# A recurrence and two feed-forward layers on one core: weights joined in place, five buffers for unit inputs, and eight units' u term on the matrix engine

## The chip, the cores and the metric

One NeuronCore of one Trainium2 chip. The metric is device time in microseconds (us) of one launch. Engines are named TensorE (PE; PEld is its weight load), VectorE (DVE), ScalarE (ACT), GpSimd (POOL) and SyncE (SP), which issues most DMAs.

## What is computed

A recurrence over 768 steps for 4 batches and 8 heads of width 48, then two feed-forward layers over the 3072 tokens (384 to 2048 to 384), the first gated by a leaky ReLU with a slope per column, the second by h * relu6(h + 3) / 6.

```python
def _attn_ref(r, k, v, w, u):
    ...
    for t in range(S):
        cur = np.einsum('bhd,bhe->bhde', u[None] * kt, vt)
        y[:, :, t] = np.einsum('bhd,bhde->bhe', rt, state + cur)
        state = wt[:, :, :, None] * state + np.einsum('bhd,bhe->bhde', kt, vt)

def _moe_ref(x, w_in, w_out, alpha):
    h = x @ w_in
    g = np.maximum(h, 0.0) + alpha * np.minimum(h, 0.0)
    return g @ w_out
```

r, k, v, w and u are fp32. The four weight matrices arrive as 64-bit floats and are turned into 32-bit ones on the chip. The u term of a step is, per head, the number sum_d(r*u*k) times the vector v.

## The kernel before

The tokens are cut into 12 thirds of 256 (three to a batch), and each third into four units, one for each pair of heads: 48 units. A unit (`add_unit`) loads a tile `un` with k, r and w (112 rows: two heads at rows 0 and 64), scans the decays backward (`scan_t`, L662) and forward (`scan_g`, L676), scales k and r by them into `kr` (`scaled`, L697), and on TensorE forms the triangle products A = k by r in two chunks of 128 (L752) and transposes of k (L760), all in `pa`. The transposes are copied out (`kt`, L791), multiplied by v (`kv`, L798 and L802) and added into the state Y (`newstate`, L847, L849). `state` (L824 on ScalarE, L826 on VectorE) puts scaled states into block-diagonal tiles `sbd`; two kinds, state0 and state1. The tile X starts as four diagonal matrices that hold the u term (`diag`, L735: four scalings of the identity), and a masked copy (`triangle`, L776, L781) overwrites the strict triangle with A. The output y of a unit is then `pc`: sbd by r (L878) and X by v (L885, L889), in the one PSUM bank `y`. `hi_` (L914, ScalarE) rounds y to fp32r and `lo_` (L920, VectorE) takes the rest. The fourth unit of a third lands in `x3`, and six `spread` DMAs (L930) lay its rows into the token tile `xt`.

The diagonal numbers come from `add_third`: for each third, two chunks of tokens of r and k are loaded (`rk`), multiplied with each other and with u (`weigh_tokens`, L606, two products for each chunk) and summed by head (`red`, L613).

The feed-forward layers run as slots (`add_slot`): 2 layers x 6 token blocks of 512 x 16 blocks of 128 hidden columns, 192 slots. A slot has nine matmuls for h and nine for the output (`mm3`, L1135 to L1137: each product is three fp32r ones, high by high, high by low, low by high), and between them q (ScalarE), the gate pg (VectorE), the rounded g (`ghi`, L1190, ScalarE) and its rest (`glo`, L1193). A block of 512 tokens needs two thirds, so slot 0 needs units 0 to 7, called early, slot 16 needs units 8 to 15, and so on.

Weights (`add_weights`) come one or two 128x384 blocks at a time; the first layer's 32 are made ready in 18 such steps during the first 16 slots and before, 14 of them with two blocks. `signed_weight_steps`: `rest` (L122) puts the top bits of the low words into the persistent tile `wa`, `sign` (L126) writes a byte of it, `join` (L129) combines it with the shifted high words into `wb`; then `hi` (L1099) rounds and `lo` (L1103) subtracts.

What sets the order: nothing is issued in program order. A `Plan` collects all operations with allowed engines (a table of costs), a due time (in slots), what they need, and buffers. `run` walks a simulated clock and issues, of the operations that can start first, the one due first, so it fixes both the engine and the order. `URGENCY` shifts due times by kind and stage and may name one engine (stages by due time: 0 below -0.5, 1 to 16, 2 to 32, 3 to 80, 4 to 95, 5); `GROUPS` shifts single units, thirds and weight steps, `SINGLE` single operations. `pair` marks operations which the plan doesn't let run beside GpSimd. Until the first slot, TensorE is filled with `warm` matmuls (L1007), up to 400, where nothing real is ready; they are left out after the first slot has begun. At the end each output block is drained from `acc` and stored (`add_drain`, L1237, L1235); the very last one in two halves, VectorE (L1246) and ScalarE (L1244), and the last three stores are issued by ScalarE (L1250).

Of the kernel before, what the change touches and what calls it, by code (L numbers as in the profile page):

```python
# [49 lines left out]
def rwkv_moe_moe2(  # L50
# [20 lines left out]
    with ExitStack() as es:  # L71
        fast_path(es, tc, unit, tok, vch, ub, w1, w2, alpha, out, flag, alp, x2d)
# [19 lines left out]
def weight_steps(nc, a, b, raw):  # L92
# [21 lines left out]
def signed_weight_steps(nc, a, b, raw):  # L114


    top, low = weight_bits(raw)
    ends = raw.bitcast(I16).rearrange("p (n four) -> p n four", four=4)[:, :, 3]

    def rest():  # L120
        low16 = a.bitcast(U16).rearrange("p (n two) -> p n two", two=2)[:, :, 0]
        nc.scalar.activation(low16, low, AF.Copy, scale=0.9373 * 2.0**-29)  # L122

    def sign():
        byte = a.bitcast(F8).rearrange("p (n four) -> p n four", four=4)[:, :, 3]
        nc.scalar.activation(byte, ends, AF.Copy, scale=-SIGN, bias=-1024.0 * SIGN, saturate=False)  # L126

    def join():
        nc.vector.scalar_tensor_tensor(  # L129
            out=b, in0=top, scalar=3, in1=a, op0=ALU.logical_shift_left, op1=ALU.bitwise_xor  # L130
        )

    return rest, sign, join


def weight_range(nc, v, raw):
# [8 lines left out]
    "add_drain.drain": {2: (-2.0, "DVE"), 3: (2.0, "ACT")},  # L145
    "add_drain.store": {2: (-6.75, None), 3: (-0.25, None)},
    "add_range.upper": {4: (2.5, None)},
    "add_slot.gate": {1: (-4.5, None), 2: (-3.0, None), 3: (-2.25, None)},
    "add_slot.ghi": {1: (-4.25, None), 2: (-5.0, None), 3: (-10.75, None)},
    "add_slot.glo": {1: (-1.5, "DVE"), 2: (3.75, None), 3: (-3.75, None)},  # L150
    "add_slot.h_": {1: (4.0, None), 2: (-4.0, None), 3: (-6.75, None), 4: (-1.0, None)},
    "add_slot.pq": {1: (-6.5, None), 2: (1.25, None), 3: (1.25, None)},
    "add_third.load_rk": {0: (1.25, None), 1: (-6.0, None), 2: (-2.25, None), 3: (-3.75, None)},
    "add_third.load_v": {0: (-4.5, None), 1: (-0.5, None), 2: (1.25, None), 3: (-5.75, None)},
    "add_third.red": {0: (-2.0, None), 1: (-4.25, None), 2: (7.0, None), 3: (-7.0, None)},
    "add_unit.add_output.hi_": {0: (-3.5, None), 1: (-6.75, None), 2: (3.25, None), 3: (-8.75, None)},
    "add_unit.add_output.lo_": {0: (-0.5, None), 1: (-2.75, None), 2: (-6.5, None), 3: (5.25, None)},
    "add_unit.add_states.newstate": {0: (-14.25, None), 1: (-4.5, None), 2: (-1.0, None), 3: (6.0, None)},
    "add_unit.check": {2: (-5.5, None), 3: (-7.25, None)},
    "add_unit.diag": {0: (-5.25, None), 1: (3.25, None), 2: (-5.25, None), 3: (-9.75, None)},  # L160
    "add_unit.keep": {0: (-0.25, None), 1: (4.75, None), 2: (-3.25, None), 3: (-18.0, None)},
    "add_unit.kt": {0: (-8.75, None), 1: (0.75, None), 2: (-6.5, None), 3: (-3.25, None)},
    "add_unit.kv": {0: (-4.5, None)},
    "add_unit.load": {0: (-3.25, None), 1: (-6.75, None), 2: (-5.75, None), 3: (3.75, None)},
    "add_unit.pa": {0: (-8.25, None), 1: (-2.75, None)},
    "add_unit.recip": {0: (-0.25, None), 1: (-3.25, None), 2: (8.5, None)},
# [1424 lines left out]
```

## Time and profile before

| what | us |
|---|---|
| median of 3 runs | 929.18 (927.97 to 929.4) |
| the profiled run, its own time | 927.52 |
| span of its profile, first to last instruction | 925.7 |
| granted TensorE clock over the span | 0.997 |
| busy in the span: PE / DVE / ACT / POOL | 915.4 / 553.6 / 520.3 / 121.6 |

The profile is one execution, recorded instruction by instruction. Views are named in words: the page's groups by line (busy time, mean of one, idle time of that engine just ahead of them), the timeline, and a table of engine time by stage. A PE row counts the warm matmuls too.

### The profile page before, as it was taken

How to read it: one execution, taken by the hardware profiler on the slowest of the kernel's cores; microseconds unless marked ns; L12 is line 12 of the kernel's file. 1: busy time of each engine (PE TensorE's matmuls, PEld its weight loads, DVE VectorE, ACT ScalarE, POOL GpSimd, SP SyncE). 2: the span in 40 equal slices, each digit the busy share in tenths (PEclk: the TensorE clock that was granted, in tenths of full speed). 3: DMA queues.
4: the chain of work that ended last, by engine and by line, in shares of the span. 5: the costliest groups of instructions: out<-in, count | busy, mean ns of one | idle time of the engine just before them, and what ended most of it. 6: DMA issues, size and time to landing. Idle time of an engine off the chain costs nothing.

```text
span 925.7 us, 13674 instructions
## 1 busy us (share of the span) xinstructions
PE 915.4 (99%) x4988; PEld 752.2 (81%) x4988; DVE 553.6 (60%) x1064; ACT 520.3 (56%) x1172; POOL 121.6 (13%) x109
## 2 busy tenths in 40 slices
PE   8999999999999999999999999999999999999997
PEld 6877888888888888888888888888888888888885
DVE  8999988766878556753357775353353443443432
ACT  5989964546545545453459996363463553543331
POOL 4321120011021231310021241000000000000000
PEclk9999999999999999999999999999999999999999
DMA  9888323222423312110145630160240330420101
GB/s 281 260 267 288 92 76 99 71 65 79 117 65 105 105 29 58 31 44 10 35 139 202 199 108 1 37 198 1 89 146 1 116 120 1 150 85 1 36 1 37
DMA packets 39629, 88.98 MB, mean 96 GB/s; under 512 B 5248, under 2 KB 10368, under 8 KB 39552
## 3 DMA queue, kind: packets, MB, share of 16 engines
q1 hardware_dynamic: 39120, 87.22, 30.2%
q8 instruction: 41, 0.67, 0.3%
q10 hardware_dynamic: 432, 0.79, 0.2%
q14 instruction: 36, 0.29, 0.1%
HBM read 76.19 MB, written 9.44 MB: 93 GB/s over the span
## 4 chain that ended last, share of the span: by engine, by line
PE 98%; DMA 1%; DVE 0%; ACT 0%; POOL 0%; issue 0%; ACTq 0%; DVEq 0%
PE acc L1135 14%; PE h L1135 14%; PE acc L1136 14%; PE acc L1137 14%; PE h L1137 14%; PE h L1136 14%; PE A L752 3%; PE warm L1007 2%; PE y L885 2%; PE y L878 2%; PE A L760 2%; DMA un<-in_unit 1%; PE y L889 1%; PE y L798 0%; PE A L798 0%; PE y L802 0%
## 5 line engine op out<-in xcount | busy, mean ns | idle before, releaser
L1135 PE MATMUL acc<-g,w 128*128 128x512 f32 x576 | 226.6, 393 | 0.0
L1136 PE MATMUL acc<-g,w 128*128 128x512 f32 x576 | 224.3, 389 | 0.0
L1137 PE MATMUL acc<-g,w 128*128 128x512 f32 x576 | 224.3, 389 | 0.0
L1190 ACT ACTIVATE g<-pg 128x512 fp32r<-128x512 f32 x192 | 120.7, 628 | 128.0 <-PE acc L1137 105.6
L1193 DVE TENSOR_TENSOR g<-pg,g 128x512 fp32r<-128x512 f32 x141 | 99.9, 709 | 132.9 <-ACT g L1190 132.6
L1135 PEld LDWEIGHTS acc<-g,w 128*128 128x128 f32 x576 | 108.6, 188 | 22.7 <-issue 0.6
L1137 PEld LDWEIGHTS acc<-g,w 128*128 128x128 f32 x576 | 108.1, 188 | 22.7
L1136 PEld LDWEIGHTS acc<-g,w 128*128 128x128 f32 x576 | 108.2, 188 | 21.8 <-DVE g L1193 0.3
L1184 DVE SCALAR_TENSOR_TENSOR pg<-q,h 128x512 f32<-128x512 f32 x96 | 65.8, 685 | 96.6 <-ACT q L1175 96.5
L1193 POOL TENSOR_TENSOR g<-pg,g 128x512 fp32r<-128x512 f32 x51 | 73.6, 1443 | 364.2 <-ACT g L1190 251.5
L1175 ACT ACTIVATE q<-h,three 128x512 f32<-128x512 f32 x96 | 65.8, 686 | 96.3 <-PE h L1137 96.2
L1135 PE MATMUL h<-xt,w 128*128 128x512 f32 x288 | 114.4, 397 | 0.0
L1137 PE MATMUL h<-xt,w 128*128 128x512 f32 x288 | 112.2, 390 | 0.0
L1136 PE MATMUL h<-xt,w 128*128 128x512 f32 x288 | 112.2, 390 | 0.0
L1135 PE MATMUL h<-x,w 128*128 128x512 f32 x288 | 112.0, 389 | 0.0
L1136 PE MATMUL h<-x,w 128*128 128x512 f32 x288 | 112.0, 389 | 0.0
L1137 PE MATMUL h<-x,w 128*128 128x512 f32 x288 | 112.0, 389 | 0.0
L1173 ACT ACTIVATE q<-h,nal 128x512 f32<-128x512 f32 x96 | 65.7, 686 | 77.1 <-PE h L1137 70.2
L1180 DVE SCALAR_TENSOR_TENSOR pg<-h,q 128x512 f32<-128x512 f32 x96 | 65.8, 686 | 37.8 <-ACT q L1173 23.0
L735 ACT ACTIVATE X<-ident,p 128x128 f32<-128x128 f32 x192 | 60.6, 390 | 11.7 <-PE y L889 11.3
L1135 PEld LDWEIGHTS h<-xt,w 128*128 128x128 f32 x288 | 54.4, 189 | 11.8 <-DVE pg L1180 0.8
L1137 PEld LDWEIGHTS h<-xt,w 128*128 128x128 f32 x288 | 54.0, 188 | 11.5
(102 smaller groups left out, 1234.0 us busy)
## 6 DMA issues: line engine op xcount, KB each, us to landing
wraw<-in_w SPq DMA_DIRECT2D x64, 384.0 KB, 5.5
un<-in_unit SPq DMA_DIRECT2D x48, 337.3 KB, 3.5
raw<-in_w SPq DMA_DIRECT2D x32, 384.0 KB, 3.3
rk<-in_tok SPq DMA_DIRECT2D x24, 384.0 KB, 4.0
v<-in_vch SPq DMA_DIRECT2D x12, 384.0 KB, 4.2
x2d<-st SPq DMA_DIRECT2D x18, 256.0 KB, 2.2
x2r<-x2d SPq DMA_DIRECT2D x18, 256.0 KB, 5.1
out<-st SPq DMA_DIRECT2D x15, 256.0 KB, 2.2
```

The lines of the kernel that those rows point to most:

```text
L735: nc.scalar.activation(X[:, i], ident, AF.Copy, scale=pp[:, i : i + 1])
L752: nc.tensor.matmul(A[h][:, cs], kr[r0 : r0 + D, 0, cs], kr[r0 : r0 + D, 1, cs], start=True, stop=True,)
L760: nc.tensor.transpose(T[:, c, :], kr[:, 0, c * C : (c + 1) * C], ident[0:PR, 0:PR])
L1135: nc.tensor.matmul(ps, whi, xhi, start=start, stop=False, skip_group_check=True)
L1136: nc.tensor.matmul(ps, whi, xlo, start=False, stop=False, skip_group_check=True)
L1137: nc.tensor.matmul(ps, wlo, xhi, start=False, stop=stop, skip_group_check=True)
L1173: nc.scalar.activation(q, k["h"], AF.Relu, scale=nal[:, f : f + 1])
L1175: nc.scalar.activation(q, k["h"], AF.Relu, bias=three)
L1180: nc.vector.scalar_tensor_tensor(out=p, in0=k["h"], scalar=0.0, in1=k["q"], op0=ALU.max, op1=ALU.subtract)
L1184: nc.vector.scalar_tensor_tensor(out=p, in0=k["q"], scalar=6.0, in1=k["h"], op0=ALU.min, op1=ALU.mult)
L1190: nc.scalar.activation(k["g"][:, 0], k["p"], AF.Copy)
L1193: eng[e].tensor_tensor(out=k["g"][:, 1], in0=k["p"], in1=k["g"][:, 0].bitcast(F32), op=ALU.subtract)
```

## The change

- Weights: `wa` and its two buffers are gone. `rest` writes its number over the low word of each 64-bit pair in the raw tile, `sign` writes byte 3 of it there, and `join` reads that low word as its second operand.
- Unit inputs have five buffers instead of three.
- Units 0 to 7 (`early`): thirds 0 and 1 load no `rk` and run no L606 and L613; no diagonal is built, X is one of three zeroed tiles. `bonus` forms r*u*k of a unit on VectorE, two small matmuls in `pa` sum it by head into PSUM (`pick` has a column for each head), `weigh_v` multiplies v by these sums on VectorE, and four matmuls with the identity in `pc` add the result to y. The low half: a matmul with minus the identity (`less`) subtracts the rounded y in PSUM, and ScalarE copies out what is left.
- More engines to choose from: `keep`, `kt`, `diag`, `ghi` and the weights' `hi` may run on VectorE too.
- Last token block of the second layer: the matmuls of the last two slots are ordered by output block, the last block is drained whole, all three on ScalarE.
- The plan's tables are replaced: `URGENCY` (with an engine named for far more kinds), `GROUPS`, `SINGLE` (615 entries become 45), and some of its costs.

The diff, cut to its core:

```diff
 def signed_weight_steps(nc, b, raw):
+    words = raw.bitcast(I32).rearrange("p (n two) -> p n two", two=2)
+    top, low = words[:, :, 1], words[:, :, 0]
 ...
     def rest():
-        low16 = a.bitcast(U16).rearrange("p (n two) -> p n two", two=2)[:, :, 0]
-        nc.scalar.activation(low16, low, AF.Copy, scale=0.9373 * 2.0**-29)
+        nc.scalar.activation(low, weight_bits(raw)[1], AF.Copy, scale=0.9373 * 2.0**-29)
 
     def sign():
-        byte = a.bitcast(F8).rearrange("p (n four) -> p n four", four=4)[:, :, 3]
+        byte = raw.bitcast(F8).rearrange("p (n eight) -> p n eight", eight=8)[:, :, 3]
 ...
     def join():
         nc.vector.scalar_tensor_tensor(
-            out=b, in0=top, scalar=3, in1=a, op0=ALU.logical_shift_left, op1=ALU.bitwise_xor
+            out=b, in0=top, scalar=3, in1=low, op0=ALU.logical_shift_left, op1=ALU.bitwise_xor
         )
 ...
 URGENCY = {
 ...
+    "add_slot.ghi": {0: (0.0, "ACT"), 1: (1.25, "DVE"), 2: (4.0, "ACT"), 3: (1.25, None), 4: (0.0, "ACT"), 5: (0.0, "ACT")},
+    "add_slot.glo": {1: (-0.75, "DVE"), 2: (-0.25, "DVE"), 3: (0.0, "DVE")},
+    "add_unit.keep": {0: (4.25, "DVE"), 1: (0.0, "DVE"), 2: (1.0, "DVE"), 3: (7.0, "DVE"), 4: (0.0, "ACT"), 5: (0.0, "ACT")},
+    "state0": {0: (0.25, "ACT"), 1: (-3.75, "ACT"), 2: (0.0, "ACT"), 3: (-2.0, "ACT"), 4: (0.0, "ACT"), 5: (0.0, "ACT")},
+    "state1": {0: (0.0, "ACT"), 1: (3.5, "ACT"), 2: (-0.5, "ACT"), 3: (-0.75, "ACT"), 4: (0.0, "ACT"), 5: (0.0, "ACT")},
+    "weigh_tokens": {0: (-2.0, "POOL"), 1: (1.25, "DVE"), 2: (5.0, "DVE"), 3: (-2.5, None)},
 ...
+    pick = const.tile([PR, 2], F32, name="pick")
+    minus = wp.tile([PR, PR], F32R, tag="w15_1", name="minus")
+    zeroed = [gp_.tile([P, 4, C], F32, tag="g", name=f"X{i}") for i in range(3)]
-    wa = [const.tile([P, 2 * DM], I32, name=f"wa{i}") for i in range(2)]
 ...
+        if 4 * t < AHEAD:
+            return
         pb = plan.buf("p", 2)
 ...
-        ub_ = plan.buf("unit", 3)
+        ub_ = plan.buf("unit", 5)
 ...
+        def bonus(e):
+            x = ap_.tile([P, 4, C], F32, tag="X", bufs=2, name=f"rp{n}")
 ...
+            u["X"] = zeroed[n % 3]
+            nc.vector.scalar_tensor_tensor(
+                out=u["ruk"], in0=u["in"][:, TH : 2 * TH], scalar=udt[:, pr : pr + 1],
+                in1=u["in"][:, 0:TH], op0=ALU.mult, op1=ALU.mult,
+            )
+        def weigh_v(e):
+            nc.vector.tensor_tensor(
+                out=u["pv"],
+                in0=v_t[t][:, :, c0 : c0 + 2 * D].rearrange("p c (h d) -> p c h d", h=2),
+                in1=u["pp"][:, :, :, None].broadcast_to([P, 2, 2, D]), op=ALU.mult,
+            )
 ...
+                for c in range(2):
+                    nc.tensor.matmul(
+                        pp[:, c, :], u["ruk"][:, c * C : (c + 1) * C], pick, start=True, stop=True
+                    )
 ...
+            for c in range(2 if early else 0):
+                cs = slice(c * C, (c + 1) * C)
+                for h, r0 in ((0, 0), (1, 64)):
+                    nc.tensor.matmul(
+                        y[r0 : r0 + D, cs], u["pv"][:, c, h, :], ident,
+                        start=False, stop=True, skip_group_check=True,
+                    )
 ...
+            def less(e):
+                nc.tensor.matmul(
+                    u["y"], minus, parts()[0], start=False, stop=True, skip_group_check=True
+                )
             def lo_(e):
                 hi, lo = parts()
+                if early:
+                    nc.scalar.activation(lo, u["y"], AF.Copy)
+                    return
 ...
-            nc.scalar.activation(k["g"][:, 0], k["p"], AF.Copy)
+            copy(e, k["g"][:, 0], k["p"])
 ...
+            at = s + 3.5 + 0.01 * i
+            if m == 1 and j == NB - 1 and f >= NF - 2:
+                at = s + NF - 1 - f + 3.5 + 0.3 * i + 0.01 * (f - NF + 2)
 ...
-        if final and i == NK - 1:
-            o = [
-                plan.op({e: 0.42}, due, lambda e, c=c: half(e, c), [o_o], new=[sb], use=[ab])
-                for c, e in enumerate(("DVE", "ACT"))
-            ]
-        else:
-            o = [plan.op({"ACT": 0.6, "DVE": 0.69}, due, drain, [o_o], new=[sb], use=[ab])]
+        by = {"ACT": 0.6} if final else {"ACT": 0.6, "DVE": 0.69}
+        o = plan.op(by, due, drain, [o_o], new=[sb], use=[ab])
```

`copy(e, out, in_)` is an activation copy on ScalarE or a `tensor_copy` on VectorE. A path for inputs out of range (`general_path`) changes as well; it does not run here.

## Rows read from the trace of the kernel before

**Rows 1.** Stages: length; busy us (count) of PE, PEld, DVE, ACT, POOL; clock; DMA; GB/s.
```profile
0.00:4.40 4.40, 3.05 (x15) 2.04 (x15) 2.86 (x11) 1.28 (x1) 3.02 (x14) 1.00 0.60 176
4.40:44.80 40.40, 37.99 (x396) 30.21 (x395) 37.50 (x92) 30.61 (x102) 14.98 (x20) 0.96 0.91 278
44.80:50.80 6.00, 6.00 (x65) 4.67 (x64) 4.94 (x9) 5.25 (x12) 1.72 (x1) 1.00 0.54 159
50.80:129.90 79.10, 79.10 (x475) 62.69 (x473) 75.13 (x143) 73.00 (x153) 12.62 (x11) 1.00 0.63 201
129.90:919.30 789.40, 789.30 (x4045) 652.54 (x4044) 432.73 (x812) 409.79 (x908) 89.22 (x64) 1.00 0.24 75
```

**Rows 2.** Groups by line, TensorE, 0 to 50.8: count | busy us, mean ns | idle before.
```profile
L1007 PE MATMUL warm<-ident 128*128 128x256 bf16 x202 | 28.4, 293 | 1.4 <-POOL ident L548 1.4
```

**Rows 3.** Timeline, all engines, 40 to 51: start us, us, instruction.
```profile
43.22 0.36 ACT L914 ACTIVATE x<-y 112x256 fp32r<-112x256 f32 x1
...
44.35 0.41 DVE L920 TENSOR_TENSOR x<-y,x 112x256 fp32r<-112x256 f32 x1
...
44.78 3.78 SPq L930 DMA_DIRECT2D xt<-x  x6
...
50.81 0.47 PE L1135 MATMUL h<-xt,w 128*128 128x512 f32 x1
```

**Rows 4.** Groups by line, TensorE, 50.8 to 129.9.
```profile
L1135 PE MATMUL h<-xt,w 128*128 128x512 f32 x48 | 19.4, 405 | 0.0
```

**Rows 5.** Groups by line, VectorE (DVE), 4.4 to 44.8.
```profile
L606 DVE TENSOR_TENSOR rk<-rk 128x384 f32<-128x384 f32 x6 | 3.7, 620 | 0.0
L606 DVE TENSOR_TENSOR rk<-rk,u_sb 128x384 f32<-128x384 f32 x6 | 3.2, 538 | 0.0
L613 DVE TENSOR_REDUCE p<-rk 128x8 f32<-128x384 f32 x6 | 3.3, 544 | 0.1
L849 DVE SCALAR_TENSOR_TENSOR Y<-Y,tg,A 112x48 f32<-112x48 f32 x12 | 3.1, 256 | 0.2
L826 DVE TENSOR_SCALAR sbd<-Y,tg 48x48 f32<-48x48 f32 x6 | 2.6, 430 | 0.0
L920 DVE TENSOR_TENSOR xt<-y,xt 112x256 fp32r<-112x256 f32 x6 | 2.5, 414 | 0.0
```

**Rows 6.** Groups by line, ScalarE (ACT), 4.4 to 44.8.
```profile
L735 ACT ACTIVATE X<-ident,p 128x128 f32<-128x128 f32 x40 | 12.3, 388 | 0.0
L824 ACT ACTIVATE sbd<-Y,tg 48x48 f32<-48x48 f32 x20 | 6.6, 329 | 2.9 <-DVE Y L847 2.5
L914 ACT ACTIVATE xt<-y 112x256 fp32r<-112x256 f32 x6 | 2.3, 385 | 0.4 <-PE y L885 0.2
```

**Rows 7.** Timeline, 8.9 to 10.2.
```profile
8.98 0.64 POOL L697 TENSOR_TENSOR kr<-un,tg 112x256 f32<-112x256 f32 x1 [1.88 <-DVE tg L662]
9.02 1.01 DVE L606 TENSOR_TENSOR rk<-rk 128x384 f32<-128x384 f32 x1
```

**Rows 8.** Groups by line, ScalarE and VectorE, 50.8 to 129.9.
```profile
L1190 ACT ACTIVATE g<-pg 128x512 fp32r<-128x512 f32 x16 | 10.0, 627 | 1.4 <-DVE pg L1180 1.4
...
L826 DVE TENSOR_SCALAR sbd<-Y,tg 48x48 f32<-48x48 f32 x10 | 2.4, 239 | 0.1
```

**Rows 9.** Groups by line and shape, weight steps, whole span.
```profile
L122 ACT ACTIVATE wa<-wraw 128x768 uint16<-128x768 uint32 x28 | 30.0, 1077 | 0.1
L129 DVE SCALAR_TENSOR_TENSOR wb<-wraw,wa 128x768 int32<-128x768 int32 x28 | 27.3, 974 | 1.5 <-ACT wa L126 1.4
L1099 ACT ACTIVATE w<-wb 128x768 fp32r<-128x768 f32 x28 | 23.4, 836 | 0.1
```

**Rows 10.** Timeline, 918 to 925.7, the end.
```profile
919.29 0.42 DVE L1246 TENSOR_SCALAR st<-acc 128x256 f32<-128x256 f32 x1
919.77 0.38 ACT L1244 ACTIVATE st<-acc 128x256 f32<-128x256 f32 x1 [5.97 <-DVE st L1246]
920.19 0.34 ACTq L1250 DMA_DIRECT2D out<-st  x1
```

More of the change, by code (lines that the diff above doesn't have):

```diff
@@ L180 @@
[L180 to L187 removed]
+    "add_slot.gate": {2: (-1.75, None), 3: (2.0, None)},
@@ new lines @@
+    "add_weights.rest": {0: (-2.5, None)},
+    "join": {0: (-6.25, None), 1: (1.5, None)},
+    "load_alpha": {0: (-5.25, None)},
+    "load_u": {0: (8.0, None)},
+    "load_ud": {0: (0.5, None)},
+    "negate": {0: (-6.0, None)},
+    "output": {0: (8.0, None), 1: (-1.5, None)},
+    "scale": {0: (3.25, None), 1: (0.75, None), 2: (0.75, None), 3: (-3.25, None)},
+    "scale_half": {0: (-5.0, "POOL")},
+    "second": {1: (1.25, None), 2: (-1.0, None), 3: (-0.5, None), 4: (2.0, None)},
+    "sign": {0: (-4.0, None), 1: (0.75, None)},
@@ new lines @@
+    "third2": -0.25,
+    "third3": -2.5,
+    "third5": -0.25,
+    "third6": -2.5,
+    "third7": 1.0,
+    "third8": -1.5,
+    "unit0": -1.75,
+    "unit1": -1.75,
+    "unit10": 1.0,
+    "unit11": -0.5,
+    "unit12": -0.25,
+    "unit13": -0.5,
+    "unit14": 1.5,
+    "unit15": -2.5,
+    "unit16": 1.25,
+    "unit17": 1.5,
+    "unit18": 0.5,
+    "unit19": -2.0,
+    "unit2": -0.5,
+    "unit20": -1.75,
+    "unit21": 0.5,
+    "unit22": -1.5,
+    "unit23": -0.25,
+    "unit25": 1.0,
@@ L409, in step @@
         else:
-            d = o["where"][e] * (2 if e == "PE" and t < self.COLD else 1)
+            d = o["where"][e]
+            if e == "PE" and t < self.COLD:
+                d = d + 0.1 if o.get("filler") else 2 * d
             if e == "PE" and state["began"] and t - state["PE"] > self.LULL:
@@ L515, in fast_path, with copy @@
     plan = Plan()
+    def copy(e, out, in_):
+        if e == "ACT":
+            nc.scalar.activation(out, in_, AF.Copy)
+        else:
+            nc.vector.tensor_copy(out, in_)
     ident = const.tile([P, P], F32, name="ident")
@@ L813, in add_unit @@
             )
-            o_tri = plan.op({"DVE": 0.73}, d - 1.5, triangle, [o_kv, o_x], use=abufs + [xb])
+            o_tri = plan.op(
+                {"DVE": 0.73}, d - 1.5, triangle, [o_kv] + ([] if early else [o_x]),
+                new=[xb] if early else [], use=abufs + ([] if early else [xb]),
+            )
         sb = [plan.buf("sbd", 4), plan.buf("sbd", 4)]
@@ L1109, in add_weights @@
         o_l["parts"] = n
-        o = plan.op({"ACT": 0.18 + 0.45 * n}, due - 0.2, rest, [o_l], new=[ab, bb], use=[wb])
+        o1 = plan.op(
+            {"ACT": 0.18 + 0.45 * n}, due - 0.2, lambda e: steps()[0](), [o_l], use=[wb],
+            kind="add_weights.rest",
+        )
         o = plan.op(
-            {"ACT": 0.18 + 0.45 * n}, due - 0.2, lambda e: k["steps"][1](), [o], use=[wb, ab],
+            {"ACT": 0.18 + 0.45 * n}, due - 0.2, lambda e: steps()[1](), [o1], use=[wb],
             kind="sign",
@@ L1384, in general_path @@
     nc.vector.memset(win[:, D : D + 1], 1.0)
-    three = gp.tile([P, 1], F32, name="gthree")
-    nc.vector.memset(three, 3.0)
     udt = gp.tile([PR, NPAIR], F32, name="udt")
```

328 lines of the change are left out of this document (159 added, 169 removed), and 76 rows, old and new, of the table SINGLE.

## The prediction

> **What bounds the kernel now.** I read a table of engine time by stage first, then the rows around the first matmul of the feed-forward part, last the groups of VectorE and ScalarE in the early stages. TensorE is busy in nearly all of every stage [rows 1], but that is no peak: before 50.8 us the largest group on it is 202 warm matmuls, which multiply the identity and are thrown away, 28.4 us by the records [rows 2]. The first real matmul, slot 0, starts at 50.81 [rows 3]. From there to 919.3 TensorE is busy throughout [rows 1], with no idle time ahead of the real matmuls in the first 16 slots [rows 4]. So the time is three pieces: a prologue of 50.8, a packed stretch of 868.5, and a tail of 6.4 after the last matmul. Work on another engine counts only where it moves the start of slot 0, makes TensorE wait behind it, or lies in the tail.
>
> What sets the prologue: between 4.4 and 44.8 VectorE is busy 37.5 of 40.4 us, ScalarE 30.6, GpSimd 15.0 [rows 1]. VectorE's last step for unit 7 (the low half of y, L920) starts at 44.35; the six spread DMAs of its third go out from 44.78 on, and slot 0 begins 6.03 us after the first of them [rows 3]. VectorE's list for eight units, then some 6 us of spreading, make the 50.8.
>
> The packed stretch hangs on less than it seems. From 50.8 to 129.9 the first 16 slots run (48 = 3 x 16 of each h matmul [rows 4]); VectorE is busy 75.1 of these 79.1 us, ScalarE 73.0. In the long rest, 129.9 to 919.3, VectorE needs little more than half [rows 1]. A shorter prologue is kept only if the 79 us of feeding follow.
>
> **VectorE before slot 0, removed.** Thirds 0 and 1 are no longer weighed and summed: four of the six token chunks in the rows, of 3.7 + 3.2 + 3.3 us, so 6.8. Eight low halves go from L920 to ScalarE, 8 x 0.41 = 3.3. The six L826 instructions, three state pairs, go to ScalarE, since both their kinds now name it in every stage: 2.6. The four products of third 2 go to GpSimd, which their kind names in stage 0: 4 of 12 in 6.9, 2.3 [rows 5]. Together 15.0.
>
> **Added there**, none of it in the trace: per unit the product r*u*k (112x256) lies between the 0.41 of L920 at that size and the 0.54 of a 128x384 product; 0.43, nearest to L920. The weighting of v (128x192) lies between the 0.26 of L849 (48 columns) and that 0.41; 0.34, in the middle as its width is. The copy L673 of two columns lies between nothing and the 0.26 of L849; 0.20, near L849, since so small a step is mostly fixed cost [rows 5]. Eight units: 8 x 0.97 = 7.8, ends 5.4 and 9.7. Net -7.2. The fill of a 128x512 tile in the setup is put at nothing: VectorE has 1.5 us free before 4.4 [rows 1], when the first input lands. Without that cover it would cost about what other one-input steps of its size do, 0.7 at most.
>
> **The chain behind VectorE.** Unit 7 needs VectorE last for its mask step (L776) and then for the low half; the high half of y starts on ScalarE at 43.22 and takes some 0.36, and the low half then waits to 44.35 in VectorE's queue [rows 3], 0.8 after its data. With the change y has four more matmuls (I put them at 0.45), then a subtracting matmul (0.3), then a low half on ScalarE as long as the high one, 0.38 [rows 6]. The 0.75 added are about the 0.8 that goes: even. These 6 us of new matmuls (8 x 0.75) take the place of warm ones, whose 28.4 are their cover.
>
> **The others before slot 0.** ScalarE loses 32 of 40 identity scalings (12.3 x 0.8 = 9.8); it gains eight low halves (3.0) and three state pairs (6 x 0.33 = 2.0) [rows 6]. GpSimd gains four products. The trace shows what that can do: a VectorE product at 9.02 that began 0.04 after a GpSimd instruction of 0.64 took 1.01 [rows 7], not 0.54, so each may hold VectorE for 0.5, in all 2.0; I take it whole. The Trainium skill (SBUF — State Buffer, Who interferes with whom) calls this a full block by whichever of the two issues first. By that rule one such wait could reach a whole GpSimd product, where the row has half a microsecond, and the loss could be double. DMA: four chunk loads of 384 KB go and two more unit buffers let inputs run ahead; I count nothing for it.
>
> Slot 0 thus starts 7.2 - 2.0 = 5.2 earlier, at 45.6. Low end: 9.7 added, 2.0 lost, 3.3. High end: 5.4 added, nothing lost, 9.6.
>
> **Feeding slots 0 to 15.** The plan moves work here too. The rounded g (L1190) of slots 0 to 14 goes to VectorE. Such a copy isn't in the trace: the one-input 128x256 step at 919.29, 0.42 with half the columns [rows 10], is the lower end, two thirds of a 128x768 two-input join, 0.65 [rows 9], the upper; 0.45, near the lower, since one input is read and none of it from PSUM: 6.8. L673 comes, 9 x 0.2 = 1.8; ten state steps leave, -2.4: +6.2 [rows 8]. Over 4.4 to 129.9 VectorE was busy 37.5 + 4.9 + 75.1 = 117.5 of 125.5 us, 8.0 idle [rows 1]. Now it has 117.5 - 7.2 + 6.2 = 116.5, and with slot 16 5.2 earlier 120.3 us for them: 3.8 idle. It fits if waits stay short. ScalarE gets room: 15 x 0.63 = 9.4 go (g), 10 x 0.33 = 3.3 come (states) [rows 6, 8].
>
> **Weights in place.** The low words and the sign byte are written into the raw tile at a step of eight bytes, and the join reads its second operand so. On VectorE the join with one stepped operand of 128x768 takes 0.97, less than twice a plain 128x384 product (1.08) [rows 5, 9]: nothing. On ScalarE the stepped read takes 1.08, the plain copy 0.84 [rows 9]; if a stepped write cost that 0.24 again, 28 x 0.24 + 8 x 0.12 = 7.7, a little over the 6.1 that ScalarE gets back and as much as it had idle besides. I take 0. The Trainium skill (SBUF — State Buffer, Door 1: The DMA port swizzle) lets fp32 step by up to four within its 16-byte lines for free. By that rule the form costs 0 and the 0.24 of the row has another cause.
>
> **Tail.** The last tile drains in two halves, one after the other (919.29 and 919.77), and its store is issued at 920.19 [rows 10]. Whole on ScalarE it takes about the 0.63 of L1190 at that size [rows 8] from 919.29 and goes out near 919.95: -0.3 rounded; ends 0 and -1, as the earlier tiles now finish sooner.
>
> **Sum.** 925.7 - 5.2 - 0.3 = 920.2 us of span. The profiled run took 927.5, the median of the runs is 929.18; the same 5.5 off the median gives 923.7.
>
> **Rivals.** (a) VectorE's 8.0 idle are waits for others and stay, so slot 16 comes only 117.5 - 116.5 = 1.0 earlier: 929.2 - 1.0 - 0.3 = 927.9, half way to it 925.8. For: VectorE is nearly full. Against: inputs get buffers, and ScalarE, for which it waits, gets room.
> (b) No change: the first weights, the y bank or an input takes VectorE's place ahead of slot 0; only the tail is left, 928.9. Against: VectorE's idle time from 4.4 to 44.8 is 2.9 in all, so nothing else held it for long.
> (c) Slower: as (a), and VectorE's new work in slots 0 to 14 is dear, g at 0.65 (+3.0) and joins 0.24 longer (14 x 0.24 + 4 x 0.12 = 3.8): 927.9 + 6.8 = 934.7. With the idle kept it turns slower once that extra passes 1.3. Against: the join row.
>
> **How the numbers follow.** Less than 0.2% (1.9 us) can't be told from no change in a measurement of this kernel. Forecast, 3.3 to 9.9 off: 0.62; (a) 0.17, of which 0.15 clears the 0.2%; (b) 0.11; (c) 0.10. Faster 0.77, same 0.13, slower 0.10. The range runs from the high end of the shift with a little of the tail (929.2 - 9.6 - 1.0 = 918.6) through (a) to near (b), 928.5; about 0.2 lie outside, (c) and most of (b) above.
>
> **What would show it.** Slot 0 at 44 to 47 with fewer warm matmuls and VectorE still full ahead of it; no idle ahead of the real matmuls in slots 0 to 15 (idle there behind g or a join is (a) or (c)); the ScalarE weight steps still near 1.08, the join near 0.97, g on VectorE near 0.45; the last store near 0.7 after the last matmul's end. A start near 50 would make the prediction wrong, and so would one near 45 with gaps behind it.

## The result, and the profile after

The changed kernel takes 939.28 us (median of 5 runs, 938.39 to 939.55), the kernel before, run beside it, 929.4 (927.97 to 931.1): a ratio of 1.0107, 95% interval 1.0097 to 1.0118. It is 1.1% slower, where 923.7 and faster had been forecast. The profiled execution of after took 939.55 us with a span of 937.7, 12.0 more than before's 925.7.

The table of engine time by stage, with the columns of [rows 1]:

```profile
0.00:4.40 4.40, 3.04 (x15) 2.17 (x16) 3.14 (x16) 1.28 (x1) 3.06 (x15) 1.00 0.53 141
4.40:44.80 40.40, 39.97 (x442) 32.60 (x441) 31.20 (x82) 25.72 (x61) 18.33 (x24) 1.00 0.92 263
44.80:50.80 6.00, 5.70 (x61) 4.60 (x60) 4.03 (x12) 5.86 (x18) 2.43 (x2) 1.00 1.03 338
50.80:129.90 79.10, 77.26 (x489) 60.21 (x489) 74.21 (x138) 70.37 (x133) 9.92 (x8) 1.00 0.54 172
129.90:919.30 789.40, 787.20 (x4028) 648.82 (x4027) 430.61 (x785) 427.08 (x951) 90.43 (x73) 1.00 0.24 76
```

VectorE's share of 4.4 to 44.8 fell from 37.50 to 31.20 [rows 1], which looks like what the forecast wanted. But this stretch no longer holds all the work ahead of slot 0. From 4.40 to the spread of unit 7's third, at 51.45, VectorE is busy 35.88 us; in before it was 37.48 up to that spread, at 44.78. The granted TensorE clock is 1.00 in every stage, where before had 0.96 in the second, so the loss is not one of clock. The DMA engines stayed as busy as before there (0.92 against 0.91) and became full from 44.8 to 50.8 (1.03 against 0.54). ScalarE fell early, but from 129.9 on it rose from 409.79 to 427.08. TensorE has gaps that it did not have: 1.84 us in the fourth stage (none before), 2.20 in the last (0.10 before).

Slot 0, in the timeline from 49 to 58 (columns of [rows 3]), with the high and low half of y for unit 7 and the spread of its third:

```profile
49.87 0.38 ACT L923 ACTIVATE x<-y 112x256 fp32r<-112x256 f32 x1
...
51.04 0.39 ACT L935 ACTIVATE x<-y 112x256 fp32r<-112x256 f32 x1
51.45 3.87 SPq L951 DMA_DIRECT2D xt<-x  x6
...
57.48 0.49 PE L1162 MATMUL h<-xt,w 128*128 128x512 f32 x1
```

It begins at 57.48, where before had 50.81 [rows 3]. The high half comes at 49.87 and not at 43.22. From the high half on the two kernels take about as long (7.6 us each), so the loss lies ahead of it.

The groups by line and shape of the weight steps, over the whole span, which answer to [rows 9] (count | busy us, mean ns | idle before):

```profile
L131 ACT ACTIVATE wraw<-wraw 128x768 fp8e5<-128x768 int16 x28 | 54.4, 1944 | 0.0
...
L127 ACT ACTIVATE wraw<-wraw 128x768 int32<-128x768 uint32 x28 | 25.4, 916 | 0.1
...
L131 ACT ACTIVATE wraw<-wraw 128x384 fp8e5<-128x384 int16 x8 | 8.6, 1073 | 0.0
...
L136 DVE SCALAR_TENSOR_TENSOR wb<-wraw 128x768 int32<-128x768 int32 x28 | 26.6, 952 | 14.1 <-ACT wraw L131 14.1
```

The row of the sign byte in before:

```profile
L126 ACT ACTIVATE wa<-wraw 128x768 fp8e5<-128x768 int16 x28 | 30.2, 1079 | 0.1
```

The sign byte (L131) takes 1.94 us for 128x768, where before's L126 took 1.08. The first step takes 0.92 against 1.08, and the join 0.95 against 0.97 [rows 9]. The join now waits 14.1 us for the sign byte, in the same row where before waited 1.4.

Two pieces of the chain of work that ended last (start us, us, what) show where that goes, and its shares by engine and by line sum it up:

```profile
75.66 1.97 ACT wraw L131
...
85.40 1.94 ACT wraw L131
```
```profile
PE 83%; ACT 13%; issue 2%; DVE 1%; DMA 1%; SPq 0%; POOL 0%; ACTq 0%; DVEq 0%; POOLq 0%
PE h L1162 12%; PE h L1164 12%; PE h L1163 12%; PE acc L1162 12%; PE acc L1164 12%; PE acc L1163 12%; ACT wraw L131 4%; PE A L734 3%; PE y L887 2%; PE warm L1028 2%; ACT wraw L127 2%; PE y L880 2%; ACT w L457 2%; ACT wv L1056 1%; PE A L742 1%
```

In before that chain was 98% TensorE. Now ScalarE is 13% of it, and 8 of these 13 points are the weight steps L131, L127 and L457. The longest gap of TensorE in the first 16 slots ends behind such a byte (timeline, 97.5 to 101):

```profile
97.59 1.91 ACT L131 ACTIVATE wraw<-wraw 128x768 fp8e5<-128x768 int16 x1
...
99.71 0.33 ACT L457 ACTIVATE kT<-A 128x224 f32<-128x224 f32 x1
...
100.09 0.26 PE L797 MATMUL A<-v,kT 128*64 128x48 f32 x1 [1.67 <-ACT kT L457]
```

The copy of the transposes stands in ScalarE's queue behind the byte (and a rounding of y, L923), and TensorE waits for it.

The early path's own instructions on VectorE from 4.4 to 44.8 (which answer to the groups that left, [rows 5]), and on TensorE over the whole span:

```profile
L694 DVE SCALAR_TENSOR_TENSOR rp<-un,udt 112x256 f32<-112x256 f32 x8 | 3.9, 487 | 1.3 <-PE y L898 1.3
L459 DVE COPY fall<-tg 112x2 f32<-112x2 f32 x9 | 3.5, 393 | 0.0
L700 DVE TENSOR_TENSOR rp<-v,A 128x192 f32<-128x192 f32 x8 | 2.8, 351 | 3.6 <-ACT kT L457 3.2 <-PE A L749 0.2
```
```profile
L1028 PE MATMUL warm<-ident 128*128 128x256 bf16 x187 | 26.8, 292 | 1.4 <-POOL ident L500 1.4
L898 PE MATMUL y<-ident,rp 128*48 128x128 f32 x64 | 4.9, 273 | 0.0
L749 PE MATMUL A<-pick,rp 112*128 112x2 f32 x32 | 4.1, 234 | 0.0
L928 PE MATMUL y<-xt,minus 112*112 112x256 f32 x6 | 2.2, 364 | 0.3 <-ACT xt L923 0.3
```

Records of matmuls overlap. By the distance from each start to the next, the new ones (L749, L898, and L928 with two more of another shape) take 3.0 + 3.7 + 1.6 = 8.3 us, while the warm ones went from 202 [rows 2] to 187, 15 of about 0.109: 1.6 us. And VectorE, no longer full, waits for ScalarE (3.2) and TensorE (1.3) ahead of these products.

The end of the timeline, which answers to [rows 10], and the last matmul of before:

```profile
930.60 0.39 PE L1164 MATMUL acc<-g,w 128*128 128x512 f32 x1
...
931.18 0.60 ACT L1265 ACTIVATE st<-acc 128x512 f32<-128x512 f32 x1 [0.47 <-PEq L80]
931.81 0.34 ACTq L1271 DMA_DIRECT2D out<-st  x1
```
```profile
918.86 0.39 PE L1137 MATMUL acc<-g,w 128*128 128x512 f32 x1
```

The drain in one piece takes 0.60. From its start to the store's issue are 0.63, against 0.90 from the first half's start before; but from that issue to the end of the span are 5.9 against 5.5. From the start of the last matmul to the end are 7.1 against 6.8: the tail lost 0.3.

### The profile page after: what moved, and what is told of

The parts are those of the page before. It is cut to its first block, busy times and chain, and to the rows that moved or that the text cites. A ratio compares the mean times of both kernels' runs of the same rounds, so it can differ in the third digit from the quotient of the medians.

```text
span 937.7 us, 13849 instructions
## 1 busy us (share of the span) xinstructions
PE 924.8 (99%) x5077; PEld 757.7 (81%) x5077; DVE 545.9 (58%) x1034; ACT 534.3 (57%) x1166; POOL 124.2 (13%) x121
## 4 chain that ended last, share of the span: by engine, by line
PE 83%; ACT 13%; issue 2%; DVE 1%; DMA 1%; SPq 0%; POOL 0%; ACTq 0%; DVEq 0%; POOLq 0%
PE h L1162 12%; PE h L1164 12%; PE h L1163 12%; PE acc L1162 12%; PE acc L1164 12%; PE acc L1163 12%; ACT wraw L131 4%; PE A L734 3%; PE y L887 2%; PE warm L1028 2%; ACT wraw L127 2%; PE y L880 2%; ACT w L457 2%; ACT wv L1056 1%; PE A L742 1%
## 5 line engine op out<-in xcount | busy, mean ns | idle before, releaser
L1220 DVE TENSOR_TENSOR g<-pg,g 128x512 fp32r<-128x512 f32 x175 | 123.5, 707 | 109.4 <-ACT g L457 108.2
L457 ACT ACTIVATE g<-pg 128x512 fp32r<-128x512 f32 x146 | 92.1, 631 | 97.8 <-PE acc L1164 88.8
L655 POOL TENSOR_TENSOR kr<-un,tg 112x512 f32<-112x512 f32 (+1 forms) x52 | 54.1, 1042 | 295.8 <-DVE tg L634 176.0
L1162 PEld LDWEIGHTS h<-xt,w 128*128 128x128 f32 x288 | 54.4, 189 | 14.8 <-DVE pg L1207 3.8
L1162 PEld LDWEIGHTS h<-x,w 128*128 128x128 f32 x288 | 54.1, 188 | 12.4 <-DVE pg L1211 1.3
```

The costliest lines, as they stand in the source:

```text
L457: nc.scalar.activation(out, in_, AF.Copy)
L655: eng[e].tensor_tensor(out=u["kr"][:, i].rearrange("p a (c s) -> p a c s", c=2), in0=u["in"][:, 0 : 2 * TH].rearrange("p (a c s) -> p a c ...
L1162: nc.tensor.matmul(ps, whi, xhi, start=start, stop=False, skip_group_check=True)
L1220: eng[e].tensor_tensor(out=k["g"][:, 1], in0=k["p"], in1=k["g"][:, 0].bitcast(F32), op=ALU.subtract)
```

## The experiments

Starts of h matmuls in the timelines of single profiled executions, in us, for the runs whose place of loss matters:

| kernel | slot 0 | slot 16 | slot 191 | span |
|---|---|---|---|---|
| before | 50.81 | 129.94 | 908.89 | 925.7 |
| after | 57.48 | 136.56 | 920.62 | 937.7 |
| word (after, sign as a whole word) | 56.45 | 133.50 | 912.74 | 929.6 |
| old_inplace (before, weights in place) | 55.72 | 137.84 | 920.62 | 937.1 |
| early_old (before, u term on TensorE) | 64.36 | 146.15 | 920.86 | 937.9 |

Each ratio below is to runs of the kernel before on the same chip in the same set.

**Theory 1: the sign byte, written into the raw tile at a step of eight bytes, is the loss.** Its rival is the early path. Two runs take the parts singly.

*word*: the sign goes out as a whole 32-bit word over the low word, in the same place; the rest's bits are thereby left out of what is joined.

```diff
-        byte = raw.bitcast(F8).rearrange("p (n eight) -> p n eight", eight=8)[:, :, 3]
+        word = low
...
-            byte, ends, AF.Copy, scale=-SIGN, bias=-1024.0 * SIGN, saturate=False
+            word, ends, AF.Copy, scale=-SIGN, bias=2.0**30
```

> The changed kernel with one form altered: sign writes a whole 32-bit word over the low word instead of one byte in it, so the order of every engine's list stays as it was (the weights lose their signs and low bits, so the numbers that come out differ). Theory 1 (the byte written into the raw tile is dear, 1.94 us where the plan has 1.08, and ScalarE's list runs late by it): sign falls to about 0.95, slot 0 starts at 51 to 54 instead of 57.5, and the time at 927 to 932. Theory 2 (the early units' longer chain and the new order are late by themselves, the byte only fills idle time): slot 0 stays at 55 or later, time 936 or more.

Measured: 930.97 us, ratio 1.003 (1.002 to 1.004). The group by line and shape:

```profile
L131 ACT ACTIVATE wraw<-wraw 128x768 int32<-128x768 int16 x28 | 25.2, 902 | 0.0
```

The same elements, read the same way and written to the same places, take 0.90 instead of 1.94, and the time falls: by 0.77% of before, 7.2 us, when each is set against before in its own set, and by 8.3 us when the two medians are subtracted. Slot 0 moves by only 1.0 (56.45): most of the sign byte's cost is paid behind it. In the table, word gains 2.0 on after from slot 0 to slot 16 and 4.8 from there to slot 191. All of these 4.8 lie between slots 80 and 112, which take 136.7 us in after and 131.9 in word; 18 of the 36 sign steps run there, for the second layer. From 476 us to 569 the chain of work that ended last goes mostly through ScalarE in after, with L131 as its largest part (21%), and through TensorE alone in word.

*old_inplace*: the kernel before, in its own order, with nothing changed but that the weights are joined in the raw tile.

```diff
-        nc.scalar.activation(low16, low, AF.Copy, scale=0.9373 * 2.0**-29)
+        nc.scalar.activation(lowi, low, AF.Copy, scale=0.9373 * 2.0**-29)
...
-        byte = a.bitcast(F8).rearrange("p (n four) -> p n four", four=4)[:, :, 3]
+        byte = raw.bitcast(F8).rearrange("p (n eight) -> p n eight", eight=8)[:, :, 3]
```

> The kernel before, with its own order, and only the weights joined in place as in the change (nothing else of it). Theory 1: sign takes 1.94 here too, rest 0.92; in the first layer that is 14 x 0.70 + 4 x 0.35 = 11 us more on ScalarE, which had 6 idle over slots 0 to 15, so 3 to 9 us slower than before: 932 to 938. Theory 2: hidden, 929 to 931.

Measured: 938.13 us, ratio 1.0099 (1.008 to 1.0119).

```profile
L126 ACT ACTIVATE wraw<-wraw 128x768 fp8e5<-128x768 int16 x28 | 54.4, 1942 | 0.0
```

This part alone, in an order that was not made for it, is as slow as the whole change. By the ratio it costs 9.2 us. By the table (11.4 of span in these two executions) it costs 4.9 ahead of slot 0, 3.0 in slots 0 to 15 and 3.8 behind. On ScalarE the two steps together take 92.6 us (54.4 + 25.2 + 8.5 + 4.5) where before has 70.4.

*join_in_wb*: the change, but the low word, sign and join in the separate tile of the joined weights, so that the byte lies at a step of four.

```diff
-        byte = raw.bitcast(F8).rearrange("p (n eight) -> p n eight", eight=8)[:, :, 3]
+        byte = b.bitcast(F8).rearrange("p (n four) -> p n four", four=4)[:, :, 3]
...
-            out=b, in0=top, scalar=3, in1=low, op0=ALU.logical_shift_left, op1=ALU.bitwise_xor
+            out=b, in0=top, scalar=3, in1=b, op0=ALU.logical_shift_left, op1=ALU.bitwise_xor
```

> The changed kernel, with rest, sign and join working in the tile wb (whole words at a step of four bytes, the byte written at a step of four, join in place), which needs no tile wa and gives the right weights; wb is now taken from rest on, which changes the plan a little. Theory 1: sign back to about 1.08, rest about 0.9, time 925 to 931. Theory 2: 935 or more.

Measured: 933.89 us, ratio 1.0058 (1.004 to 1.0077), 0.49% or 4.6 us less than after by the ratios (5.4 by the medians), but not under before.

```profile
L130 ACT ACTIVATE wb<-wraw 128x768 fp8e5<-128x768 int16 x28 | 30.3, 1080 | 0.1
```

The byte is back at 1.08. The expected time was missed: the tile is now taken earlier, the plan came out a little different, and slot 0 began at 59.83.

*forms*: after, with six of each form of write set behind the end, to tell the step from the width and from sharing a tile.

> The changed kernel with a bench after its end: six instructions of each form on 128x768, ScalarE with a 64-bit stepped source, VectorE joins, and a VectorE copy of 128x512. Theory 1a (the slow thing is a byte at a step of eight, wherever): 1.9 in the raw tile and in a tile apart, 1.08 at a step of four. Theory 1b (the slow thing is writing into the tile that is read): 1.9 in the raw tile at either step, 1.08 apart. Whole words at a step of eight 0.92 in both. VectorE join 0.95 with either second operand, copy of 128x512 0.44.

The timeline of ScalarE behind the end (start us, us, instruction, count; "fraw" is also the tile that is read, "fapart" another; L110 writes the sign byte, L113 the first step's product; the six bytes at 965.04 lie at a step of four bytes, the others shown at eight):

```profile
951.19 1.95 ACT L110 ACTIVATE fapart<-fraw 128x768 fp8e5<-128x768 int16 x1
952.89 1.95 ACT L110 ACTIVATE fraw<-fraw 128x768 fp8e5<-128x768 int16 x1
...
965.04 6.51 ACT L110 ACTIVATE fraw<-fraw 128x768 fp8e5<-128x768 int16 x6
971.58 11.56 ACT L113 ACTIVATE fraw<-fraw 128x768 uint16<-128x768 uint32 x6
983.17 11.56 ACT L113 ACTIVATE fapart<-fraw 128x768 uint16<-128x768 uint32 x6
994.76 5.41 ACT L113 ACTIVATE fraw<-fraw 128x768 int32<-128x768 uint32 x6
```

Bytes at four take 6.51 / 6 = 1.08, half words at eight 11.56 / 6 = 1.93 whether into the tile that is read or into another, and whole words at eight 5.41 / 6 = 0.90. The byte at eight, 1.95 into either tile, goes with them. So the cost, on ScalarE, belongs to a write smaller than a word at a step of eight bytes. The tile has no part in it, and neither has the step alone.

*old_word_rest*: the kernel before, where the first step writes its half word at a step of four, with the whole word written instead.

```diff
-        low16 = a.bitcast(U16).rearrange("p (n two) -> p n two", two=2)[:, :, 0]
-        nc.scalar.activation(low16, low, AF.Copy, scale=0.9373 * 2.0**-29)
+        word = a
+        nc.scalar.activation(word, low, AF.Copy, scale=0.9373 * 2.0**-29)
```

> The kernel before with one edit: the first weight step writes its product as a whole 32-bit word where it wrote the lower half word at a step of four bytes. Theory 1a (what costs is a write smaller than a word at a step): the step falls from 1.08 to 0.90 us on ScalarE, 2.9 us less of ScalarE in the first layer's weights; time 926 to 928.5 if ScalarE's list reaches slots 0 to 15, within 0.2% of before if it does not. If the width of the written element has no part in it: 1.08 as before and the time unchanged.

Measured: 928.89 us, ratio 0.9998 (0.9986 to 1.001).

```profile
L122 ACT ACTIVATE wa<-wraw 128x768 int32<-128x768 uint32 x28 | 25.0, 898 | 0.0
```

The step falls from 1.08 to 0.90 as theory 1 says, and the time stays: 5.7 us less on ScalarE over the span (5.0 in this row, 0.7 in the smaller shape) are worth nothing here, while 22 more cost 9.2 in old_inplace. So the 0.24 that the prediction saw between the stepped first step and a plain copy (1.08 against 0.84 [rows 9]) was for the most part the half-word write and not, as it was read, a stepped operand.

**Theory 2: what is left (+2.8 us in word, where 5.5 less had been forecast) is the early path.** Its matmuls are not covered. A rival is the new tables of the plan, which place everything else anew; no run has them without the early path.

*early_old*: the kernel before, in its own order, with the u term of the eight early units on TensorE and their low half by subtraction, as in the change; weights and buffers as before.

```diff
+            u["ruk"] = x[0:PR, 0:TH]
...
+            nc.vector.scalar_tensor_tensor(
+                out=u["ruk"], in0=u["in"][:, TH : 2 * TH], scalar=udt[:, pr : pr + 1],
```

> The kernel before, in its own order, with one part of the change alone: the eight early units' u term goes through the matrix engine (pick and pv matmuls, the zeroed tiles, the low half by subtraction), weights and the units' buffers stay as they were. Theory 2 (the path adds some 8 us of real matmuls ahead of slot 16, start to start in the trace of after, and warm ones do not shrink to match): 932 to 936, slot 0 later than 50.8, TensorE's warm total within 2 us of before's 21.9. The prediction's mechanism (VectorE's list bounds the prologue and warm matmuls cover the new ones): 921 to 928, slot 0 at 46 to 49.

Measured: 940.11 us, ratio 1.0123 (1.0102 to 1.0144), more than either theory said. The chain ahead of slot 0 shows why:

```profile
40.63 0.48 DVE rk L551
41.20 7.23 DMA un<-in_unit
48.46 0.69 DVE tg L609
```

The load of a unit input goes out at 41.20, behind two products of VectorE, and the chain waits for it until 48.46, when the unit's first scan begins. There are three buffers for these inputs, and in the early path the r*u*k product reads one of them late. Whether that is it, the next run asks.

*word_bufs3*: word with three buffers for unit inputs instead of five.

```diff
-        ub_ = plan.buf("unit", 5)
+        ub_ = plan.buf("unit", 3)
```

> The kernel with the change and the sign written as a whole word (930.97), with three buffers for unit inputs again instead of five; the plan places the loads and what follows them anew for that. In the kernel before with the u term alone on TensorE (940.11) the chain held a unit load of 7.23 us that went out only when a buffer came free. If the early path needs the two more buffers (they are freed later, by the r*u*k product): 934 to 941, with unit loads on the chain ahead of slot 0. If they are of no use: 930 to 932.

Measured: 938.69 us, ratio 1.0115 (1.0094 to 1.0136), 7.7 more than word; slot 0 at 61.62. Loads of unit inputs are again 15% of the chain ahead of slot 0, where word's is TensorE nearly throughout. So in this order the two more buffers are worth that much. The plan was made anew for three, and no run has five without the early path, so it is not shown that the early path alone makes them worth it. Their room does not hang on the dear byte: join_in_wb has no tile `wa` and five buffers too.

*word_nopv*: word without the four u-term matmuls of each early unit and without the subtracting one, 5.3 us of TensorE by start-to-start times.

```diff
-            for c in range(2 if early else 0):
+            for c in range(0):
```

> The kernel with the change and the sign written as a whole word (930.97), without the four u-term matmuls of each early unit and without the low-half subtraction on TensorE: the u term and that subtraction are left out of what is computed, the order of all else is kept. If the new matmuls lie in time that TensorE spends on warm ones or idle anyway (the prediction's cover): 930 to 931.5, no change. If they stand in the way of slots 0 to 15 (theory 2): 925.5 to 928.5, 5.3 us of matmuls less most of it.

Measured: 928.05 us, ratio 0.9993 (0.9981 to 1.0004), 2.9 less than word, and by the ratios 0.37%, 3.4. (Its profiled execution, 930.86, was the longest of ten, so no row of it is read.) So of the 5.3 us some 3 stood in the way and some 2 were covered. Without them the kernel is level with before: nothing remains of the 5.2 us that a shorter VectorE list was to bring.

*word_lesswarm*: word without 13 of the 41 warm matmuls queued ahead of the first triangle product, which were still running in after's trace when its input was ready.

```diff
+            if o.get("filler") and skip:
+                skip -= 1
+                continue
```

> The kernel with the change and the sign as a whole word (930.97), with 13 of the 41 warm matmuls that are queued ahead of the first triangle product taken out. The first product's input was ready at 6.81 and it began at 8.35 in the profile of after. If that 1.5 us delay reaches slot 0 (56.45): slot 0 at 55 to 55.5 and the time 929.5 to 930.2. If another chain sets slot 0: within 0.5 us of 930.97 (or slower, if the clock falls).

Measured: 930.58 us, ratio 1.0016 (1.0005 to 1.0027), slot 0 at 55.92. That is 0.4 to 1.3 less than word by the two ways of comparing: a part of the delay may reach the end, but it is no main cause.

**Theory 3, on the forecast's first step: does VectorE's list set slot 0 in the kernel before?** Its rivals are TensorE's fixed order with the warm matmuls in it, and the loads.

*before_lessdve*: the token products and sums of the first three thirds on VectorE, narrowed.

```diff
+                w = 8 if t < 3 and e == "DVE" else DM
...
+                    out=rk[:, 0, 0:w], in0=rk[:, 0, 0:w],
...
```

> The kernel before, same order on every engine; on VectorE the token products and sums of the first three thirds are narrowed from 384 to 8 and 32 columns a partition (most of their u term is left out of what is computed). 18 instructions of 0.62, 0.54 and 0.54 shrink to 0.1 to 0.2 each by the small steps in the trace: 10.2 us of VectorE's list ahead of slot 0 become about 3. The prediction's first step (VectorE's list bounds the prologue) wants slot 0 at 43 to 46 and 922 to 925. If the prologue is a chain through several engines with warm matmuls put at fixed places (theory 3): slot 0 at 48.5 to 50.8 and 927 to 929, with VectorE idle instead.

Measured: 928.31 us, ratio 0.9997 (0.9986 to 1.0008), slot 0 at 51.76. The row of the stage table for 4.4 to 44.8, then two groups of VectorE there:

```profile
4.40:44.80 40.40, 38.28 (x388) 30.39 (x387) 30.03 (x89) 29.61 (x98) 13.93 (x20) 1.00 0.98 267
```
```profile
L853 DVE SCALAR_TENSOR_TENSOR Y<-Y,tg,A 112x48 f32<-112x48 f32 x12 | 3.1, 259 | 3.1 <-PE A L806 3.1
...
L851 DVE COPY Y<-A 112x48 f32<-112x48 f32 x4 | 0.8, 207 | 3.4 <-PE A L806 3.4
```

7.5 us of VectorE's list are gone (30.03 against 37.50 [rows 1]) and nothing moved. The time turned into waits of VectorE for TensorE. Before, the same L849 row had 0.2 of idle time [rows 5].

*before_halfwarm*: the kernel before without every second warm matmul.

```diff
+            odd += o.get("filler", False)
+            if o.get("filler") and odd % 2:
+                continue
```

> The kernel before, without every second of its 202 warm matmuls, the order of all else kept: 11 us less by start to start times. The prediction counts warm matmuls as a cover, work that fills time in which TensorE has nothing to do: then the time stays within 0.2% as long as the granted clock stays at 1.00 and idle time takes their place. Theory 3 (they stand at fixed places in TensorE's queue and hold the real ones behind them): slot 0 at 46 to 49 and 924 to 927. If the clock falls to the lower level ahead of slot 0: 930 or more, with that level in the rows.

Measured: 928.42 us, ratio 0.9995 (0.9981 to 1.0009), slot 0 at 50.77. The clock stayed at 1.00. In before the chain ahead of slot 0 is 45% warm matmuls; here it runs through loads and VectorE:

```profile
2.12 5.97 DMA un<-in_unit
8.11 0.70 DVE tg L662
...
23.51 8.83 DMA un<-in_unit
32.43 0.70 DVE tg L662
```

*word_halfwarm*: the same in word.

> The kernel with the change and the sign written as a whole word (930.97), without every second of its warm matmuls, the order of all else kept: some 10 us less by start to start times. Cover: unchanged within 0.2%. Theory 3 (fixed places, they hold the real ones): slot 0 at 52 to 54.5 against 56.45, and 926.5 to 929. More than 13 of the first 41 going gave 0.4 already.

Measured: 931.83 us, ratio 1.0037 (1.0021 to 1.0054), slot 0 at 57.24, the clock 0.87 from 4.4 to 44.8, where word has 1.00. No gain there either, but with the lower clock this run does not tell whether the warm matmuls hold anything.

So no single one of the two holds slot 0. The view of the DMA engines from 0 to 51 us in the kernel before (busy tenths in 40 slices, then packets and bytes):

```profile
DMA  0599999999999999899999953228998999994328
...
DMA packets 5402, 13.03 MB, mean 255 GB/s; under 512 B 866, under 2 KB 1378, under 8 KB 5397
```

Nearly every slice from 2.6 to 29 us is full; first-layer weights, tokens and unit inputs share it. The next three runs take away two or three of the candidates at once.

*before_both* (VectorE's part and half the warm matmuls), *before_three* (and two thirds of the bytes of six token loads) and *before_lessdma* (VectorE's part and the loads, all warm matmuls in place):

```diff
-                nc.sync.dma_start(rk_t[q], tok[t, c])
+                w = 128 if t < 3 else DM
+                nc.sync.dma_start(rk_t[q][:, :, 0:w], tok[t, c][:, :, 0:w])
```

> The kernel before with VectorE's token work narrowed as in the run without it and every second warm matmul left out, order kept (most of the first three thirds' u term is left out of what is computed). If VectorE's list and TensorE's queue only hid each other: slot 0 at 44 to 47, 922 to 926. If the loads set the prologue (theory 4): slot 0 at 50 to 52 and 927 to 929.5, with idle time on VectorE and TensorE that ends with unit loads.

> As before_both, and the token loads of the first three thirds bring 128 of 384 columns each: six loads of 384 KB become 128 KB, 1.5 MB of the 13.0 MB that the trace of before moves by 51 us, at its 255 GB/s 6 us. Theory 4 (the loads): slot 0 at 44 to 48 and 922 to 926. If the loads have no part: as before_both, within 0.2%.

> As before_three, but with all 202 warm matmuls in their places. If the warm matmuls are a true cover: the same time as before_three within 0.2%. If they hold real matmuls once the loads come earlier: slot 0 2 to 4 later than in before_three, and 2 to 4 us more.

| kernel | us | ratio | slot 0 |
|---|---|---|---|
| before_both | 927.42 | 0.9991 (0.9976 to 1.0006) | 52.40 |
| before_three | 925.23 | 0.9962 (0.9948 to 0.9977) | 48.76 |
| before_lessdma | 928.07 | 1.0003 (0.9992 to 1.0014) | 51.36 |

Neither pair moves anything that can be told. All three together give 3.4 us, and with all warm matmuls in their places 2.8 of them are lost again, slot 0 coming 2.6 later. With VectorE's part gone, the loads and TensorE's fixed order each hold the prologue, and each hides the other. Whether VectorE's list is a third of that kind stays open: loads and warm matmuls without VectorE's part were not run.

*before_two*: the two edits of these that leave the result alone, half the warm matmuls and the whole-word first step, together in the kernel before.

> The kernel before with the first weight step as a whole word (0.18 less on ScalarE for each 128x768, nothing by itself) and without every second warm matmul (nothing by itself). If ScalarE and TensorE's queue are the pair that hides each other: 924 to 927. If the loads and VectorE's list stay the bound, as the runs with those taken away too suggest: 927 to 929.5, no change.

Measured: 929.04 us, ratio 0.9997 (0.9984 to 1.0011). No kernel here that does all of the work beats the one before by more than the noise.

## Why the prediction was wrong, step by step

**Weights in place: the step that cost most.** The prediction saw the question (does a stepped write cost?), had a bound from a row (7.7 us on ScalarE), and took 0. In old_inplace ScalarE has 22 us more, and this part alone loses 9.2 us; in the changed kernel it is 7.2 by the ratios. The bound was too low because it carried over the 0.24 of one row: in forms a half word or byte takes 0.90 as a whole word, 1.08 at a step of four bytes, 1.93 to 1.95 at eight. The first step, written as a whole word, even became cheaper (0.92), and the join's part was right: 0.952, put at no more than 0.97. By the Trainium skill (SBUF — State Buffer, Door 1: The DMA port swizzle), which the prediction set beside its 0, a step inside a 16-byte line is free. The whole words agree (0.90 at a step of eight bytes), bytes and half words do not, and the measurement decides.

**VectorE bounds the prologue: wrong.** The 31.20 in 4.4 to 44.8 comes near the 37.5 - 7.2 = 30.3 worked out, but that stretch ends 6.7 us ahead of the spread of unit 7's third. Up to that spread VectorE's work fell by 1.6 us (35.88 against 37.48), with 1.9 of weight steps of two blocks now in it. And before_lessdve shows that even a cut of 7.5 alone brings nothing. A busy share of 93% was taken for a bound. What the row left out is that the instructions of the other engines stand in fixed orders beside it. The chain of before already ran through TensorE's warm matmuls, and the DMA engines were as full (0.91 in [rows 1]). "DMA: I count nothing for it" was the other half of the same error.

**Warm matmuls cover the new ones: half wrong.** 8.3 us came where 6 were put, and the warm ones gave up 1.6, not 6. word_nopv puts what stood in the way at some 3 of 5.3 us. The "even" of the chain behind VectorE failed by half a microsecond: the four matmuls took 0.47 a unit (0.45), but from the high half to the low half are 1.17 against 1.13, where 0.8 were to go and 0.3 to come. That is small beside the 6.65 by which the high half itself is late.

**Five buffers, counted at nothing: wrong as a price.** word_bufs3 puts them at 7.7 us, in the new order and with the early path; without these they were not tried.

**Feeding slots 0 to 15: the number right, in part by luck.** It took 79.08 us from slot 0 to slot 16 after, 79.13 before. But in word it took 77.05, with TensorE busy throughout: it has 451 matmuls there, where before has 476, as some work of the units had moved ahead of slot 0. In after 1.84 us of gaps behind ScalarE made up for that. So word's 5.6 at slot 0 are only 3.6 at slot 16. g on VectorE (L459) took 0.438, put at 0.45.

**Terms on VectorE**: r*u*k 0.487 (0.43), the weighting of v 0.351 (0.34), the copy of two columns 0.393 before 44.8 (0.20). The copy is the only one that is far off, and GpSimd is the reason: see the last section. For eight units the three come to 9.8, at the high end that was given (9.7), not 7.8.

**Tail**: 0.60 for the drain (0.63), and the gain of 0.3 from the drain's start to the issue came (the prediction's own 919.95 against 920.19 is 0.24). But the drain began 0.15 later behind the last matmul (0.58 against 0.43), and 0.4 were lost behind the issue. None is left.

**The rivals.** (c) had the right side and the wrong mechanism: it laid the loss on VectorE's join and g, which were 0.952 and 0.438. (b) named "the first weights, the y bank or an input takes VectorE's place", which is near to what the runs show of the prologue; it was dismissed because VectorE had only 2.9 us idle. Two chains of about equal length look just like that: in before VectorE is 93% busy there and the DMA engines 91%.

The sum, then: -5.2 became none, and the weights in place cost 7.2 (after against word) to 9.2 us (old_inplace), both by the ratios to before. In ratios, 1.07% is 0.77% for the sign byte and 0.30% for the rest. The rest goes when the new matmuls are left out (word_nopv, 0.9993); how much of it the plan's new tables give or take stays open, and so does what bounds the prologue in the changed order.

## What to carry to other kernels

Before an in-place layout is priced at nothing, time its writes by element width and step; a write narrower than a word can cost nearly twice as much in one place as in the other (here 1.94 against 1.08). A nearly full engine is not yet the bound: ask which other chains end at the same place, and take them away together, since each alone hides behind the others. Where a change frees a resource and spends it again (a tile for two buffers), its parts have to be priced as a set.

## What the runs showed of the chip

On ScalarE, 128x768 elements into SBUF took 0.90 us as whole 32-bit words, at a step of four or eight bytes; as bytes or half words 1.08 at a step of four and 1.93 to 1.95 at eight, into the same tile or another. Words took 0.90 from int16 and from uint32 input.

A copy of 112x2 on VectorE took 0.14 with no GpSimd instruction beside it and 0.53 to 0.62 when it began within 0.3 us behind the start of a GpSimd product. In the timeline of after:

```profile
12.83 0.63 POOL L655 TENSOR_TENSOR kr<-un,tg 112x256 f32<-112x256 f32 x1 [1.35 <-DVE tg L620]
12.87 0.62 DVE L459 COPY fall<-tg 112x2 f32<-112x2 f32 x1
...
16.32 0.16 DVE L459 COPY fall<-tg 112x2 f32<-112x2 f32 x1
...
29.15 0.14 DVE L459 COPY fall<-tg 112x2 f32<-112x2 f32 x1
```

The copy ends 0.03 after the product (13.49 and 13.46); in the three other such meetings ahead of slot 0, at 4.96, 9.23 and 26.43, it was 0.02 to 0.03. So even a step of two columns waits for the whole of what is left of the product. The Trainium skill (SBUF — State Buffer, Who interferes with whom) calls this a full block by whichever issues first, and these rows agree. One row does not: at 16.32 the copy began 0.05 behind a short GpSimd step (L522, 0.26, no product) and took only 0.16. The prediction had taken half a microsecond per meeting from [rows 7] and had not counted such copies among those that meet.
